# Batch 0 of a fused attention and two-layer feed-forward kernel: VectorE in a written-out order, maxima one tile ahead

## Chip, cores and metric

One core of one Trainium2 chip runs the whole program. The metric is the device time of one execution in microseconds (us); lower is better. Before the change three runs gave 1151.52, 1152.64 and 1152.75 us, a median of 1152.64 us.

## What is computed

Attention with 4 batches, 8 heads, 576 rows and head size 64, in float32, with a threshold on the scores; then two feed-forward layers over the 2304 tokens. Cut to what matters:

```python
scores = (1/8) * q @ k.T                     # 4 x 8 x 576 x 576
m = max(scores, axis=-1)
scores = where(scores >= m - tau, scores, -1e9)
attn = exp(scores - m);  attn /= sum(attn) + 1e-9
x = attn @ v                                 # reshaped to 2304 x 512
g = x @ w_gate;  x = (g * sigmoid(g) * (x @ w_val)) @ w_out      # 512 -> 1536 -> 512
h = max(x @ w_in, 0);  out = (h * h) @ w_out2                    # 512 -> 2048 -> 512
```

## The kernel before, in words

The attention is cut into 144 tiles of 128 query rows by 576 key columns. A pair of heads has 9 tiles and a batch has 4 pairs, so tiles 0 to 35 are batch 0. The main loop (L845 to L895) makes one iteration i for each tile; each tile passes through a chain that spreads over several iterations:

- QK (L599): TensorE makes the scores into one of two PSUM buffers s0 and s1 (L603), four matmuls of 288 columns, eight for the mixed tile of a pair. QK(i+1) is issued in iteration i.
- RED (L621): VectorE takes the row maximum less tau, the threshold (tensor_scalar with an accumulator, seen as TENSOR_SCALAR_CACHE_REDUCE and DVE_READ_ACCUMULATOR, L623).
- CUT (L628): ScalarE applies the threshold (Prelu, L631) from PSUM into the single buffer z. After it the score buffer is free for QK of the tile two further on.
- EXP (L635): ScalarE takes the exponential into one of three buffers e and sums the row (L639).
- RCP (L642): VectorE takes the reciprocal of the sum (L644). NORM (L646): GpSimd multiplies e by it (L649).
- TR (L661): TensorE transposes the five 128-column blocks of e into two PSUM banks (L669). From tile 20 on all tiles use the same two banks.
- PH (L683): the two banks are copied out, in batch 0 one half by VectorE (L55) and one by ScalarE (L53). In batches 1 to 3 ScalarE copies both (L689) and VectorE takes the rest of a two-part split (PL, L701, L61).
- AV (L715): TensorE multiplies by v; in batch 0 five float32 matmuls (L725), later ten (L728), in four of nine iterations.

In iteration i, RED, CUT and EXP are those of tile i, RCP and NORM of tile i-1, TR of tile i-2, PH of tile i-3.

Two other jobs run beside the attention. `pair_steps` (L538) prepares the next pair of heads: loads and moves on the queue of SyncE (SP), two splits on ScalarE, VectorE (L565) and GpSimd. And the class `Loader` (L104) brings in the first five blocks of first-layer weights, 30 pieces of 256 columns: they lie in memory as 64-bit words and are turned into two float32 parts. A piece is a DMA on SP's queue (L128), one absolute value on ScalarE (L137), four steps on VectorE (L139, L141, L145, L147: a tensor_scalar each for the first two, a scalar_tensor_tensor for the others, 256 columns each, all in SBUF), a copy on ScalarE (L53) and a subtraction on GpSimd (L61). `loader.start()` begins a piece, from iteration 8 on in every second iteration and from 36 on in each; at most three are under way, in three buffers. `loader.tick(engine)` (L153) issues the next step of the oldest piece that waits for that engine; a change of engine within a piece needs a new iteration. The loop has four ticks for VectorE in an iteration, two for ScalarE, one for GpSimd.

When batch 0 is done, the first layer's matmuls for its rows are woven into the loop as "fill" (L788): per half batch five units of 24 matmuls (L226), each of which needs four of the 30 pieces, and then an output stage (L271), which needs the last ten pieces.

The program is written in an order, but a scheduler sorts it: each instruction has a priority by its place in the program, `tc.high_priority(offset=n)` (L842) shifts it by n instructions (the tables `early0` for iterations below 36 and `early` above, L1605 and L1612), and an engine that is free in the scheduler's own model gets the ready instruction with the best priority, be it from a later iteration. On the chip each engine then runs its instructions in that order. `tc.issue_after(x)` adds an edge: what is issued inside it comes after x on x's engine.

The parts of the loop that the change touches, as they stand before (arguments cut):

```python
    for i in range(NTILE + lag + 1):
        t = i - lag - 1
...
        at_(loader.tick, "D", name="LD")
        if i < NTILE:
            at_(RED, i); at_(CUT, i)
        if 0 <= t < NTILE:
            at_(PH, t); at_(NEG, t)
        if i < NTILE:
            at_(EXP, i)
        at_(loader.tick, "D", name="LD")
...
        if 0 <= i - 1 < NTILE:
            at_(RCP, i - 1); at_(NORM, i - 1)
        at_(loader.tick, "D", name="LD")
        at_(QK, i + 1); work(i); at_(TR, i - lag)
```

Of the kernel before, what the change touches and what calls it, by code (L numbers as in the profile page):

```python
# [20 lines left out]
B, H, S, D = 4, 8, 576, 64  # L21
# [46 lines left out]
def attention_moe(tc, qkv, qk0, tau, w1, w2, out, cfg):  # L68
    nc = tc.nc
# [103 lines left out]
    loader = Loader()  # L173
# [242 lines left out]
    for i in range(2):  # L416
        t = [ptp.tile([P, P], F32R, name=f"qt{i}{j}", tag=f"qt{i}{j}") for j in range(2)]
# [120 lines left out]
    def pair_steps(p):  # L538

        raw = load_pair(p)  # L540
        land = rawp.tile([P, 2, S], F32R, name=f"land{p}", tag="land")
        q, k = raw[:, 0:S], raw[:, S : 2 * S]
        qh, kh = land[:, 0], land[:, 1]

        def move(h):
            hd = head(h)
            rows = slice(hd["odd"] * D, (hd["odd"] + 1) * D)
            for dst, parts_ in (
                (hd["qs"], (qh, q.bitcast(F32R))),
                (hd["kh"], (kh, kh)),  # L550
                (hd["kl"], (k.bitcast(F32R), k.bitcast(F32R))),
            ):
                for j, src in enumerate(parts_):
                    nc.sync.dma_start(dst[j * D : (j + 1) * D, :].bitcast(F32), src[rows, :].bitcast(F32))
            tail(hd)

        yield None
        if cfg["qs"] == "A":
            nc.scalar.activation(qh, q, AF.Copy, scale=qscale)
        else:  # L560
            nc.gpsimd.tensor_scalar(qh, q, scalar1=qscale, scalar2=1.0, op0=ALU.mult, op1=ALU.mult)
        yield None
        ops.copy(cfg["kh"], kh, k)
        yield None
        nc.vector.scalar_tensor_tensor(  # L565
            q.bitcast(F32R), q, qscale, qh.bitcast(F32), op0=ALU.mult, op1=ALU.subtract
        )
        yield None
        ops.sub(cfg["kl"], k[:, :HS].bitcast(F32R), k[:, :HS], kh[:, :HS].bitcast(F32))
        yield None  # L570
        ops.sub(cfg["kl"], k[:, HS:].bitcast(F32R), k[:, HS:], kh[:, HS:].bitcast(F32))
        move(2 * p)
        yield None
        values(heads[2 * p], 2 * p, raw)
        yield "next"
        move(2 * p + 1)
        yield None
        values(heads[2 * p + 1], 2 * p + 1, raw)
        yield None
# [16 lines left out]
    NTILE = len(tiles)  # L596
    st = [dict() for _ in range(NTILE + 8)]
# [211 lines left out]
    def work(i):  # L809

        fstate["credit"] += cfg["rate"]
        if avq:
            at_(AV, avq.pop(0))
            if fstate["credit"] < cfg["extra"]:
                return
        if fstate["credit"] > 0:
            y = at_(fill_group)
            if y is None:
                fstate["credit"] = 0
            else:  # L820
                fstate["credit"] -= y
# [12 lines left out]
    def at_(f, *args, name=None):  # L834
        if name in ("LD", "LA") and 8 <= fstate["i"] < 16:

            with tc.issue_after(st[1]["red" if name == "LD" else "exp"]):
                return f(*args)
        off = cfg["early0" if fstate["i"] < 9 * NPAIR else "early"].get(name or f.__name__, 0)
        if not off:  # L840
            return f(*args)
        with tc.high_priority(offset=off):  # L842
            return f(*args)

    for i in range(NTILE + lag + 1):  # L845
        mp1.age += 1
        fstate["i"] = i
        t = i - lag - 1
        if i == cfg["three"] + lag:
            mp1.banks = deque(bank[2:])  # L850
        if i >= cfg["ldat"] and (i % cfg["lev"] == 0 or i >= 9 * NPAIR):
            at_(loader.start, name="LS")
        at_(loader.tick, "D", name="LD")
        if i < NTILE:
            at_(RED, i)
            at_(CUT, i)
        if 0 <= t < NTILE:
            at_(PH, t)
            at_(NEG, t)
        if i < NTILE:  # L860
            at_(EXP, i)
        at_(loader.tick, "D", name="LD")
        at_(loader.tick, "A", name="LA")
        at_(mp1.flush, "D", name="FD")
        if 0 <= t < NTILE:
            at_(PL, t)
            if tiles[t][2] in PARTS:
                avq.append(t)
        if 0 <= i - 1 < NTILE:
            at_(RCP, i - 1)  # L870
            at_(NORM, i - 1)
        at_(loader.tick, "D", name="LD")
        at_(mp1.flush, "A", name="FA")
        if i + 1 < NTILE:
            at_(QK, i + 1)
        work(i)
        if 0 <= i - lag < NTILE:
            at_(TR, i - lag)
        at_(mp1.flush, "P", name="FP")
        at_(loader.tick, "P", name="LP")  # L880
        at_(loader.tick, "A", name="LA")
        if i < NTILE:
            b, p, k = tiles[i]
            ha = b * H + 2 * p
            pr = i // 9
            if pr == 0:
                for _ in range((0, 1, 2)[k] if k < 3 else 0):
                    next(first)()
            elif k < 2:
                at_(next, steps, name="PS")  # L890
            if pr + 1 < B * NPAIR and k >= 2:
                if k == 2:
                    steps = pair_steps(pr + 1)
                at_(next, steps, name="PS")
        at_(loader.tick, "D", name="LD")  # L895
    while avq or not fstate["end"]:
        mp1.age += 1
        mp1.flush()
# [10 lines left out]
    f = 0  # L909
# [638 lines left out]
def pack(inputs):  # L1548
# [15 lines left out]
    def cols(w, nf):  # L1564
# [48 lines left out]
        "TR": 8, "LD": -21, "FD": 4, "NEG": -4, "FA": -19, "PL": -12, "PS": -25, "PH": 6, "LS": 64, "RCP": -8,  # L1613
        "FP": -40, "NORM": -25, "LP": -100,
    },
    "rate": 2600,
    "extra": 4000,
    "wl2": "D",
# [6 lines left out]
def program(arrays):  # L1625
    import concourse.bacc as bacc

    nc = bacc.Bacc("TRN2", target_bir_lowering=False, num_devices=1, dynamic_dma_scratch_size=512)
    args = [nc.dram_tensor(n, a.shape, mybir.dt.from_np(a.dtype), kind="ExternalInput").ap() for n, a in arrays]
    out = nc.dram_tensor("out_0_dram", (NT, DM), F32, kind="ExternalOutput").ap()  # L1630
    with tile.TileContext(nc) as tc:
        attention_moe(tc, *args, out, CFG)
    return nc
# [9 lines left out]
```

## Time and profile before

| | us |
|---|---|
| median of three runs | 1152.64 |
| the profiled execution | 1153.14 |
| its span, first to last instruction | 1151.3 |
| PE (TensorE matmul) busy in the span | 1115.7 (97%) |
| DVE (VectorE) busy | 874.8 (76%) |
| ACT (ScalarE) busy | 689.2 (60%) |
| POOL (GpSimd) busy | 242.8 (21%) |
| tile 9's maximum starts | 28.39 |
| tile 38's maximum starts | 109.55 |

The profile is one execution, recorded by the hardware; times count from its first instruction. An instruction of an engine can start a little before the one ahead of it ends, so durations add up to slightly more than the time they take. PE's busy time is modelled at its ends and is not PE at its peak. The granted clock of TensorE was 0.997 of full speed over the span. A busy engine is not always the bound: what matters is which engine the others wait for in that stretch.

### The profile page before, as it was taken

To read this page: it belongs to the slowest core of one execution; us is meant where nothing else is said; L and a number is where in the kernel's file an instruction comes from. 1 tells how busy PE (TensorE), PEld (TensorE's weight loads), DVE (VectorE), ACT (ScalarE), POOL (GpSimd) and SP (SyncE) were. 2 spreads that over 40 slices of the span, in tenths; PEclk is the share of its full clock that TensorE was granted. 3 is DMA by queue.
4 is the path that set the end of the run, shared out by engine and by line. 5 is a ranking of instruction groups with operands and counts; after the bars stand their busy time and mean duration, and the time that the engine had idled before them with its cause. 6 is when DMAs were issued, how large, how long until landed. Compare 5 with 4: busy or idle time off the path is not lost.

```text
span 1151.3 us, 19654 instructions
## 1 busy us (share of the span) xinstructions
PE 1115.7 (97%) x6572; PEld 1011.6 (88%) x6572; DVE 874.8 (76%) x2143; ACT 689.2 (60%) x1626; POOL 242.8 (21%) x363
## 2 busy tenths in 40 slices
PE   7888999999999999999999999989999999999998
PEld 5766989999999999998888888889898998899997
DVE  7999997877877773889986888668648767866554
ACT  7988988988888883554443444235546555543221
POOL 5565664555455531000000000000000000000000
PEclk9999999999999999999999999989999999999999
DMA  6666433443333400332220234246364445444542
GB/s 195 193 178 166 128 99 95 100 120 95 95 95 95 105 22 1 101 93 82 83 74 1 73 131 161 91 143 244 137 210 174 174 157 177 153 155 138 187 171 80
DMA packets 55827, 143.15 MB, mean 124 GB/s; under 512 B 7600, under 2 KB 8880, under 8 KB 55728
## 3 DMA queue, kind: packets, MB, share of 16 engines
q1 hardware_dynamic: 55584, 141.92, 39.8%
q8 instruction: 52, 0.85, 0.3%
q14 instruction: 47, 0.39, 0.1%
q10 hardware_dynamic: 144, 0.00, 0.0%
HBM read 93.06 MB, written 22.28 MB: 100 GB/s over the span
## 4 chain that ended last, share of the span: by engine, by line
PE 76%; DVE 12%; ACT 5%; DMA 2%; issue 2%; POOL 0%; POOLq 0%; DVEq 0%; ACTq 0%; SPq 0%
PE mm L226 17%; PE mm L1453 17%; PE mm L1400 13%; PE mm L271 8%; PE bank L226 6%; PE bank L669 4%; PE s L613 4%; PE bank L271 4%; PE bank L728 4%; DVE st__101 L623 2%; DMA wr<-in_w_dram 1%; ACT z L631 1%; DVE pt L61 1%; ACT e L639 1%; DVE xs_m L61 1%
## 5 line engine op out<-in xcount | busy, mean ns | idle before, releaser
L669 PE MATMUL bank<-ident,e 128*128 128x128 f32 x720 | 165.4, 275 | 10.2 <-DVE x L55 3.8
L649 POOL TENSOR_SCALAR e<-e,r 128x576 f32<-128x576 f32 x144 | 113.4, 787 | 148.1 <-DVE r L644 104.6
L61 DVE TENSOR_TENSOR pt<-bank,pt 128x384 fp32r<-128x384 f32 x216 | 100.3, 486 | 51.1 <-ACT pt L689 49.9
L226 PE MATMUL mm<-xs,wa 128*128 128x512 f32 (+2 forms) x672 | 125.7, 347 | 0.5 <-ACT x L53 0.5
L226 PEld LDWEIGHTS mm<-xs,wa 128*128 128x128 f32 x672 | 109.5, 188 | 15.7 <-ACT x L53 0.7
L631 ACT ACTIVATE z<-s,thr 128x576 f32<-128x576 f32 x144 | 106.8, 742 | 26.5 <-DVE st__101 L623 18.5
L623 DVE TENSOR_SCALAR_CACHE_REDUCE st__101<-s,tau_c 128x576 bf16<-128x576 f32 x144 | 116.6, 810 | 5.2 <-PE s L613 4.2
L669 PEld LDWEIGHTS bank<-ident,e 128*128 128x128 f32 x720 | 96.4, 141 | 21.7 <-DVE x L55 5.9
L226 PE MATMUL bank<-xs_m,wa 128*128 128x288 f32 x576 | 109.7, 327 | 3.7 <-DVE xF L740 1.8
L689 ACT ACTIVATE pt<-bank 128x384 fp32r<-128x384 f32 x216 | 88.7, 436 | 21.5 <-PE bank L669 20.2
L639 ACT ACTIVATE e<-z 128x577 f32<-128x577 f32 x144 | 99.6, 692 | 1.5 <-POOL e L649 0.4
L226 PEld LDWEIGHTS bank<-xs_m,wa 128*128 128x128 f32 x576 | 89.0, 189 | 7.1 <-DVE xs_m L61 2.7
L728 PE MATMUL bank<-pt,vs 128*128 128x256 f32 (+1 forms) x480 | 92.1, 323 | 2.1 <-ACT pt L689 1.4
L613 PE MATMUL s<-kh,qs 128*128 128x288 f32 x256 | 78.1, 319 | 7.4 <-ACT nident L413 5.9
L728 PEld LDWEIGHTS bank<-pt,vs 128*128 128x128 f32 x480 | 73.9, 190 | 3.8 <-ACT pt L689 2.1
L1470 DVE TENSOR_TENSOR xF<-xF,mm 128x512 f32<-128x512 f32 x54 | 37.0, 686 | 50.9 <-PE mm L1453 50.9
L226 PE MATMUL mm<-xs,wb 128*128 128x512 f32 (+1 forms) x360 | 74.9, 368 | 0.0
L613 PE MATMUL s<-kl,qs 128*128 128x288 f32 x256 | 73.7, 301 | 0.0
L226 PEld LDWEIGHTS mm<-xs,wb 128*128 128x128 f32 x360 | 62.9, 188 | 11.3
L53 ACT ACTIVATE wb<-wf 128x256 fp32r<-128x256 f32 x82 | 34.0, 414 | 64.5 <-DVE wf L1057 38.4
L1054 ACT ACTIVATE wf<-wr 128x256 f32<-128x256 f32 x64 | 27.6, 433 | 68.6 <-DMA wr<-in_w_dram 51.0
L1453 PE MATMUL mm<-wb,wx 128*128 128x512 f32 x270 | 67.1, 389 | 0.0
(156 smaller groups left out, 2603.0 us busy)
## 6 DMA issues: line engine op xcount, KB each, us to landing
wr<-in_w_dram SPq DMA_DIRECT2D x106, 256.0 KB, 2.9
raw<-in_qkv_dram SPq DMA_DIRECT2D x15, 896.0 KB, 4.7
kh<-land SPq DMA_DIRECT2D x60, 144.0 KB, 2.6
kl<-raw SPq DMA_DIRECT2D x60, 144.0 KB, 2.8
xF<-in_w_dram SPq DMA_DIRECT2D x30, 256.0 KB, 2.9
right<-kept1T SPq DMA_DIRECT2D x8, 768.0 KB, 5.3
right<-kept0T SPq DMA_DIRECT2D x7, 768.0 KB, 5.3
right<-kept SPq DMA_DIRECT2D x6, 768.0 KB, 5.1
```

The costliest lines, as they stand in the source:

```text
L61: e.tensor_tensor(out, a, b, op=ALU.subtract)
L226: mm(pt[:, :n], w[:, a, col + c * P : col + (c + 1) * P], xs[:, b, c, :], start=(i == 0), stop=(i == len(TERMS) - 1),)
L271: mm(pt[:, :n], w[:, a, 2 * DM + m * P : 2 * DM + (m + 1) * P], u[:, b, :], start=(k == 0), stop=(k == last),)
L613: mm(sp[:, cols], l, r[:, cols], start=(n_ == 0), stop=(n_ == len(pairs) - 1),)
L623: red = nc.vector.tensor_scalar(st_, st[t]["s"][:, :S], scalar1=tau_c, scalar2=None, op0=ALU.subtract, op1=ALU.max, accum_out=th)
L631: nc.scalar.activation(z[:, :S], st[t]["s"][:, :S], AF.Prelu, bias=st[t]["thr"], scale=-1.0, alpha=1 / SLOPE)
L639: ex = nc.scalar.activation(e, st[t]["z"], AF.Exp, scale=-SLOPE, accum_out=sum_)
L649: nc.gpsimd.tensor_scalar(e, e, scalar1=r, scalar2=1.0, op0=ALU.mult, op1=ALU.mult)
L669: mm(dst[:, j], e[:, c0 : c0 + P], ident, is_transpose=True, start=(j == 0), stop=(j == len(cols) - 1),)
L728: mm(o[:, :n], hd["vs"][:, SLOT[k % 5], :], pt[:, k, lo : lo + n], start=(k == 0), stop=(k == 9))
L1400: mm(bank[:, :BK], w[:, a, c * P : (c + 1) * P], t[:, b, c, :], start=(n == 0 and x in ("11", "12", "S1")), stop=(n == 5), skip_group_chec ...
L1453: mm(pt, u[:, b, s * P : (s + 1) * P], w[a], start=(half == 0 and j == 0 and i == 0), stop=(half == 1 and j == 1 and i == 2),)
```

## The change

In iterations 9 to 37 VectorE's attention and loader steps are chained by edges into one order: the reciprocal of tile i-1, the copy of tile i-3, the maximum of tile i+1, and two loader steps. NORM comes right behind the reciprocal. The other two loader ticks are left out in these iterations. The maximum moves from iteration i to iteration i-1, and for it QK of tile i+2 is issued at the end of iteration i, where QK of tile i+1 was issued in its middle. (Tiles 0 to 35 are not split in PH, so NEG issues nothing for them.)

```diff
+    order = {"after": None}
+    def inorder(f, *args, name=None):
+        if order["after"] is None:
+            at_(f, *args, name=name)
+        else:
+            with tc.issue_after(order["after"]):
+                at_(f, *args, name=name)
+        traced = nc.cur_bb.bb.instructions
+        engine = st[0]["red"].engine
+        order["after"] = next(x for x in reversed(traced) if x.engine == engine)
...
-        at_(loader.tick, "D", name="LD")
-        if i < NTILE:
-            at_(RED, i)
+        fixed = cfg["fixed"][0] <= i < cfg["fixed"][1]
+        if fixed:
+            inorder(RCP, i - 1)
+            at_(NORM, i - 1)
+            if i == cfg["fixed"][0]:
+                inorder(RED, i)
             at_(CUT, i)
-        if 0 <= t < NTILE:
-            at_(PH, t)
-            at_(NEG, t)
-        if i < NTILE:
+            inorder(PH, t)
+            inorder(RED, i + 1)
             at_(EXP, i)
-        at_(loader.tick, "D", name="LD")
+            for _ in range(2):
+                inorder(loader.tick, "D", name="LD")
+        else:
...
-        if 0 <= i - 1 < NTILE:
+        if 0 <= i - 1 < NTILE and not fixed:
             at_(RCP, i - 1)
             at_(NORM, i - 1)
-        at_(loader.tick, "D", name="LD")
+        if not fixed:
+            at_(loader.tick, "D", name="LD")
         at_(mp1.flush, "A", name="FA")
-        if i + 1 < NTILE:
+        if i + 1 < NTILE and not fixed and i != cfg["fixed"][1]:
             at_(QK, i + 1)
         work(i)
...
-        at_(loader.tick, "D", name="LD")
+        if cfg["fixed"][0] <= i + 1 <= cfg["fixed"][1]:
+            at_(QK, i + 2)
+        if not fixed:
+            at_(loader.tick, "D", name="LD")
...
+    "fixed": (9, 38),
```

The branch behind `else:` holds the old order, with RED left out in iteration 38, whose maximum iteration 37 has made.

## Rows read from the trace of the kernel before

**Rows 1.** The page's 40 slices of the span: busy tenths of two engines.
```profile
PE   7888999999999999999999999989999999999998
DVE  7999997877877773889986888668648767866554
```

**Rows 2.** Stretches of the first 190 us; the first line names the columns.
```profile
core 0: us, PE busy (x) PEld busy (x) DVE busy (x) ACT busy (x) POOL busy (x), PEclk, DMA share, GB/s
...
28.40:109.55 81.15, 69.69 (x399) 55.87 (x400) 76.37 (x199) 72.68 (x180) 48.15 (x67) 1.00 0.67 185
109.55:138.00 28.45, 27.75 (x204) 26.65 (x204) 27.11 (x76) 26.59 (x67) 17.55 (x26) 1.00 0.49 132
138.00:166.60 28.60, 25.54 (x184) 23.52 (x184) 28.14 (x71) 22.34 (x57) 18.95 (x27) 1.00 0.44 114
166.60:190.00 23.40, 22.98 (x179) 22.47 (x177) 16.28 (x44) 20.26 (x52) 10.83 (x16) 1.00 0.27 58
```

**Rows 3.** VectorE in order of time: start, duration; tile 9 to tile 38.
```profile
27.52 0.95 DVE L147 SCALAR_TENSOR_TENSOR xF<-xF 128x256 int32<-128x256 int32 x1
28.39 0.81 DVE L623 TENSOR_SCALAR_CACHE_REDUCE st__101<-s,tau_c 128x576 bf16<-128x576 f32 x1
...
64.00 0.79 DVE L623 TENSOR_SCALAR_CACHE_REDUCE st__101<-s,tau_c 128x576 bf16<-128x576 f32 x1
...
65.06 0.80 DVE L623 TENSOR_SCALAR_CACHE_REDUCE st__101<-s,tau_c 128x576 bf16<-128x576 f32 x1
...
68.69 0.81 DVE L623 TENSOR_SCALAR_CACHE_REDUCE st__101<-s,tau_c 128x576 bf16<-128x576 f32 x1
...
109.55 0.81 DVE L623 TENSOR_SCALAR_CACHE_REDUCE st__101<-s,tau_c 128x576 bf16<-128x576 f32 x1
```

**Rows 4.** ScalarE by line, 28.4 to 109.5: busy, mean ns | idle before.
```profile
L631 ACT ACTIVATE z<-s,thr 128x576 f32<-128x576 f32 x29 | 21.5, 741 | 5.4 <-DVE st__101 L623 2.8 <-DVE r L644 2.4
L137 ACT ACTIVATE xF<-xF 128x256 f32<-128x256 f32 x12 | 5.3, 441 | 0.0
L53 ACT ACTIVATE wa<-xF 128x256 fp32r<-128x256 f32 x11 | 4.5, 414 | 1.2 <-DVE xF L147 1.2
```

**Rows 5.** The loader's VectorE steps L139, L141, L145, L147 before and behind tile 38.
```profile
0.00:109.55 109.55, 9.37 (x22) 1.00 0.67 188
109.55:166.60 57.05, 3.16 (x8) 1.00 0.47 123
...
0.00:109.55 109.55, 10.70 (x22) 1.00 0.67 188
109.55:166.60 57.05, 4.18 (x8) 1.00 0.47 123
...
0.00:109.55 109.55, 14.62 (x22) 1.00 0.67 188
109.55:166.60 57.05, 6.21 (x9) 1.00 0.47 123
...
0.00:109.55 109.55, 9.83 (x21) 1.00 0.67 188
109.55:166.60 57.05, 3.88 (x9) 1.00 0.47 123
```

**Rows 6.** Loader steps alone, then one beside GpSimd's NORM, in order of time.
```profile
61.31 0.28 DVE L141 TENSOR_SCALAR wf<-wf 128x256 int32<-128x256 int32 x1
...
62.20 0.41 DVE L145 SCALAR_TENSOR_TENSOR wf<-xF,wf 128x256 int32<-128x256 int32 x1
...
67.63 0.87 POOL L649 TENSOR_SCALAR e<-e,r 128x576 f32<-128x576 f32 x1
...
67.91 0.86 DVE L145 SCALAR_TENSOR_TENSOR xF<-xF 128x256 int32<-128x256 int32 x1
```

**Rows 7.** TensorE's first fill matmul, the loader's last step, the first output matmul.
```profile
113.57 0.69 PE L226 MATMUL bank<-xs_m,wa 128*128 128x288 f32 x4
...
166.11 0.41 DVE L147 SCALAR_TENSOR_TENSOR xF<-xF 128x256 int32<-128x256 int32 x1
...
166.85 0.82 PE L271 MATMUL bank<-m_u,wa 128*128 128x288 f32 x5
```

**Rows 8.** SP's queue at the loader's DMAs: waits, ns min/median/max.
```profile
L128 SPq EVENT_SEMAPHORE  x24: 17/88/5037, 19.1 to 139.6; - x24
```

More of the change, by code (lines that the diff above doesn't have):

```diff
@@ L852, in attention_moe @@
             at_(loader.start, name="LS")
-        at_(loader.tick, "D", name="LD")
-        if i < NTILE:
-            at_(RED, i)
+        fixed = cfg["fixed"][0] <= i < cfg["fixed"][1]
[4 more added lines that the diff above has]
+                inorder(RED, i)
             at_(CUT, i)
-        if 0 <= t < NTILE:
-            at_(PH, t)
-            at_(NEG, t)
-        if i < NTILE:
+            inorder(PH, t)
+            inorder(RED, i + 1)
             at_(EXP, i)
-        at_(loader.tick, "D", name="LD")
+            for _ in range(2):
+                inorder(loader.tick, "D", name="LD")
+        else:
+            at_(loader.tick, "D", name="LD")
+            if i < NTILE:
+                if i != cfg["fixed"][1]:
+                    at_(RED, i)
+                at_(CUT, i)
+            if 0 <= t < NTILE:
+                at_(PH, t)
+                at_(NEG, t)
+            if i < NTILE:
+                at_(EXP, i)
+            at_(loader.tick, "D", name="LD")
         at_(loader.tick, "A", name="LA")
@@ L868, in attention_moe @@
                 avq.append(t)
-        if 0 <= i - 1 < NTILE:
+        if 0 <= i - 1 < NTILE and not fixed:
             at_(RCP, i - 1)
             at_(NORM, i - 1)
-        at_(loader.tick, "D", name="LD")
+        if not fixed:
+            at_(loader.tick, "D", name="LD")
         at_(mp1.flush, "A", name="FA")
-        if i + 1 < NTILE:
+        if i + 1 < NTILE and not fixed and i != cfg["fixed"][1]:
             at_(QK, i + 1)
@@ L894, in attention_moe @@
                 at_(next, steps, name="PS")
-        at_(loader.tick, "D", name="LD")
+        if cfg["fixed"][0] <= i + 1 <= cfg["fixed"][1]:
+            at_(QK, i + 2)
+        if not fixed:
+            at_(loader.tick, "D", name="LD")
     while avq or not fstate["end"]:
```

## The prediction, made before the changed kernel was run

> **What bounds the kernel now.** I read the page's 40 slices first, for the places where TensorE is not full. They are the first ten slices or so: PE stands at 7 and 8 tenths in the first four, while DVE stands at 9 in most of them, and behind the attention PE stays at 9 [rows 1]. So the kernel is bound by TensorE except early on, and time is won there alone: a microsecond less of PE's idle time early is a microsecond less at the end, as long as PE finds its work later as before.
>
> Next the stretches [rows 2]. Between the maxima of tile 9 and tile 38, the stretch that the change rewrites, 81.15 us pass for 29 tiles. PE is busy for 69.69 us of them and idle for 11.5; VectorE for 76.37, ScalarE for 72.68. Behind it the picture turns. From 109.55 to 138 PE is busy for 27.75 of 28.45 us, VectorE for 27.11. From 138 to 166.6 VectorE is busy for 28.14 of 28.60 us, PE for 25.54. Only after that does VectorE fall to 16.28 of 23.40.
>
> Then VectorE in order of time [rows 3]. The maxima come in pairs, at 64.00 and 65.06, and the next at 68.69: two tiles, then over three microseconds of other VectorE work. ScalarE, which needs the maximum for CUT, sits idle for 5.4 us in the stretch before its 29 CUTs [rows 4].
>
> What fills VectorE between the pairs is mostly the loader. Up to tile 38 its four lines have 22, 22, 22 and 21 instructions, 87 steps; behind it, to 166.6, 34 at most, one of which starts ahead of the border and is counted twice, so 33 [rows 5]. 87 + 33 = 120, the 30 pieces. The scheduler has run the loader ahead: by the program's own order 14 pieces (56 steps) are due in iterations up to 37, and it has done 87.
>
> **The change, part by part.** The sum is made against the profiled execution, 1153.14 us with a span of 1151.3; the median of three runs lies 0.5 lower. About 0.2%, 2.3 us, is what a measurement of this kernel can tell from no change.
>
> *Loader steps in a fixed order.* No step of the chained iterations can run ahead any more, and an iteration has two. Piece k starts in iteration 8 + 2(k-1), takes its absolute value two iterations on, and its four steps in the next two pairs, 12 + 2(k-1) and the one after. Thirteen pieces fit until iteration 37: 52 steps where 87 ran, 35 fewer. ScalarE loses six of the nineteen pieces it converts in the stretch, at 0.44 + 0.41 us [rows 4]: 5.1 us.
>
> *What that gives.* In the stretch VectorE has 76.37 us of work, less 22 of its 74 steps (76.37 - 22 x 0.52 = 65); ScalarE 72.68 - 5.1 = 67.6; PE its unchanged 69.69. PE is now the longest, so the stretch can't be shorter than that, and the gain at most 11.5 us. Some idle time stays: PE was idle for 1.8% of the stretch 166.6 to 190, where nobody else is full, and for 10.7% of 138 to 166.6 [rows 2]; with these ends the stretch takes 71.0 or 78.0 us. I take 6%, 74.1, nearer the middle because ScalarE at 67.6 is almost as long: 7 us gained, with ends 3 and 10. Ahead of tile 9's maximum stands a loader step from 27.52 to 28.39 that moves behind it [rows 3]: another 0.9. Together **8 us, between 3 and 11**.
>
> *What has to be paid back.* The 35 steps are not gone. The output stage of the fill needs all 30 pieces, and it starts at 166.85, right behind the loader's last step at 166.11 [rows 7]; the first fill matmul needs only four and starts at 113.57, so it is not delayed. Behind tile 38 the loader now has 68 steps in place of 33, on an engine that is 95% and 98% busy there. The price of a step: alone 0.28 or 0.41 us [rows 6], with overlapping ends about 0.27 on average; in that stretch 17.4 us for 34, 0.52 [rows 5]. I take 0.40, between them, since PE waits can open room: 14 us, between 9.5 and 18.2. Off that go VectorE's own idle 1.8 us there (57.05 - 27.11 - 28.14) and a share of the 7.1 us idle from 166.6 to 190 [rows 2], say 3, if the last pieces slip past 166.6: **9 us paid back, between 0.6 and 16.4**.
>
> *The maximum a tile ahead.* It takes away at most ScalarE's 5.4 us of waits [rows 4]; since PE sets the stretch, this is inside the 8 us, not beside it. In its place VectorE now stands at the reciprocal until EXP of the tile before has ended, and the copy of tile i-3, the next maximum and two loader steps queue behind it. VectorE has 65 us of work in some 74, so 9 us of such waiting fit; beyond that TensorE's transposes, which wait for the copies, would be late next.
>
> *QK an iteration sooner.* It is still free only once CUT has read the buffer, and on PE the order stays QK(i+2), work, TR: it stood in the middle of iteration i+1 ahead of that work and now stands at the end of iteration i. Nothing, either way; the score buffer covers it, and without that cover the maximum of the next tile would be late by one QK.
>
> *The queues.* No DMA is added. On SP's queue a loader DMA that waits for its buffer holds up the moves for the next pair behind it; 24 of the 30 have a wait, 0.088 us in the middle and 5.04 at most [rows 8]. Pieces an iteration slower can lengthen such waits; the moves are due an iteration or more later, so I count 0, with a loss of up to 5 in the range. On POOL, NORM comes right behind the reciprocal, ahead of the loader's subtraction as before: 0.
>
> *Collisions.* The same loader step takes 0.41 us alone and 0.86 beside a NORM [rows 6]. In the new order NORM falls beside the copy and the maximum. That cheapens steps inside the chained stretch, where by the sum VectorE is no longer the longest: 0 there. The Trainium skill ("SBUF — State Buffer", Who interferes with whom) has VectorE and GpSimd share a port pair as an exclusive lock, the later one waiting until the first has ended; the two durations agree. By it the 35 steps that move behind tile 38, where GpSimd is not ordered and is busy for 36.5 of 57 us, cost the upper price and the sum would be 5 us worse.
>
> The sum: 1153.1 - 8 + 9 = 1154.1, and 0.5 lower for the median: **1153.6 us**, no difference that can be measured.
>
> **The rivals.**
>
> *Faster: the debt sinks into slack.* From 109.55 to 138 PE is 97.5% busy, so VectorE's time there may not be what the end waits for; attention tiles, which need no weights, could run ahead on PE while the loader catches up, and the last pieces fall into the free 7.1 us. Then 2 us are paid back: 1152.6 - 8 + 2 = **1146.6**. For it: PE's fullness there, and that four pieces are enough to begin. Against it: VectorE is 95% and 98% busy, and the attention's own VectorE work comes first in that queue too.
>
> *Slower: the debt is dearer than the gain.* It is one mechanism, in the stretch 109.55 to 166.6: VectorE is the bound there and each of the 35 moved steps costs its full 0.52 us. 18.2 - 4.8 = 13.4 are paid for a gain of 5 to 6, PE keeping more of its idle time: about +8, **1160**. It decides from a price of (8 + 4.8) / 35 = 0.37 us a step. For it: 98% from 138 on, and the output stage starting right behind the loader. Against it: the first half of that stretch belongs to PE. The Trainium skill ("Perfetto Trace Analysis", Optimization Strategy) says that regimes with different busiest engines may gain by being interleaved; this change pulls loader work out of the one and stacks it in the other, and by that rule this rival comes true. No run here shows it yet.
>
> *The order was about the same already.* Then neither gain nor debt appears, and the time stands at 1152.6. The 87 steps against 52 speak against it; the time would be as in my forecast.
>
> **How the numbers follow.** Gain and debt nearly cancel in my sum, with errors of some 4 us in each: no change (with the last rival) 0.36, faster 0.35, slower 0.29. The likeliest case's own range is 1150.3 to 1154.9. The ends of the bounds are 1152.6 - 11 + 0.6 = 1142 and 1152.6 - 3 + 16.4 = 1166; they need all terms at one end. The range 1145.5 to 1160.5 holds the faster case with a 7 us gain and the slower one with 8, and leaves out about 2 in 10.
>
> **What would show it.** Tile 38's maximum should start at 99 to 104 us instead of 109.55, single maxima some 2.55 us apart instead of pairs, 52 loader steps ahead of it, no idle time of ScalarE for the maximum. Behind it 68 loader steps, VectorE full until the last, the output stage starting at 165 to 170. PE's idle time in the chained stretch should fall to about 4 to 5 us and rise by as much behind. I am wrong if tile 38 doesn't come earlier (the chain blocks VectorE), or if the output stage starts before 160 (the debt was hidden), or after 172 (it was dearer).

## The result and the profile after

The changed kernel is **slower**: a median of 1160.85 us against 1152.08, a ratio of 1.0084 with an interval of 1.0055 to 1.0113 (it is formed from all the runs; the quotient of the two medians is 1.0076). Run once more on another occasion it took 1163.83 against 1152.84, ratio 1.0098 (1.0079 to 1.0117). The forecast was no difference, with a range up to 1160.5.

The profiled execution after took 1166.21 us, with a span of 1164.4. It lies above the median: against the profiled execution before it loses 13.1 us, where the medians differ by 8.8, and a part of what its stretches show is TensorE's clock (last section). The page's 40 slices, as in [rows 1]:

```profile
PE   7988879999999999999999999999999999999998
DVE  5888997877778784789986978778647767866554
```

A slice is 29 us. The second has risen from 8 to 9, the fifth and sixth, 116 to 175 us, have fallen from 9 to 8 and 7: time was won early and lost right behind. To measure both, the stretches are cut where the kernel's own work cuts them: from tile 9's maximum to tile 38's, and from there to the start of the fill's output stage. In the kernel before these are 28.39 to 109.55, as in [rows 2], and 109.55 to 166.85. First that second stretch before, columns as in [rows 2]:

```profile
109.55:166.85 57.30, 53.55 (x388) 50.42 (x388) 55.50 (x146) 49.18 (x124) 36.59 (x53) 1.00 0.47 123
```

The profile after:

```profile
26.80:104.34 77.54, 68.99 (x395) 55.38 (x394) 62.86 (x175) 68.02 (x163) 40.63 (x58) 0.99 0.60 162
104.34:175.10 70.76, 59.90 (x392) 53.12 (x391) 68.78 (x174) 56.82 (x143) 44.76 (x62) 0.97 0.48 142
```

and the profile of the second occasion:

```profile
26.90:103.00 76.10, 69.00 (x399) 55.46 (x398) 62.59 (x175) 67.93 (x163) 40.54 (x58) 1.00 0.61 165
103.00:174.50 71.50, 60.55 (x388) 54.68 (x387) 69.02 (x176) 56.86 (x143) 45.35 (x62) 0.93 0.49 141
```

This is nearly the whole result. In the first stretch VectorE's busy time fell from 76.37 us to 62.86, by 13.5, and the stretch became shorter by only 3.6 (5.1 on the second occasion). In the second, VectorE has 68.78 us where it had 55.50, 13.3 more, and the stretch became longer by 13.5, from 57.3 to 70.8: VectorE is busy for 97% of it, before and after. Work was taken from an engine where it held the stretch only in part and given to it where it is nearly full. Of the 13.5 us, TensorE's idle time makes up 7.1 and its busy time 6.4. The output stage starts at 175.07 instead of 166.85:

```profile
112.03 0.56 PE L226 MATMUL bank<-xs_m,wa 128*128 128x288 f32 x3
...
177.71 0.41 DVE L147 SCALAR_TENSOR_TENSOR xF<-xF 128x256 int32<-128x256 int32 x1
...
175.07 0.56 PE L271 MATMUL bank<-m_u,wa 128*128 128x288 f32 x3
```

These are the lines of [rows 7]: the fill still begins early, 1.5 us ahead of before, but its output stage comes 8.2 us later. From there to the end 989.3 us pass, before 984.4; on the second occasion 987.1.

VectorE's maxima, as in [rows 3], mostly stand alone now: tiles 9 and 10 and tiles 11 and 12 are still 1.2 to 1.3 us apart, and from tile 13 on no two are closer than 1.8 us.

```profile
26.80 0.82 DVE L623 TENSOR_SCALAR_CACHE_REDUCE st__101<-s,tau_c 128x576 bf16<-128x576 f32 x1
...
44.08 0.81 DVE L623 TENSOR_SCALAR_CACHE_REDUCE st__101<-s,tau_c 128x576 bf16<-128x576 f32 x1
...
46.01 0.81 DVE L623 TENSOR_SCALAR_CACHE_REDUCE st__101<-s,tau_c 128x576 bf16<-128x576 f32 x1
...
48.73 0.82 DVE L623 TENSOR_SCALAR_CACHE_REDUCE st__101<-s,tau_c 128x576 bf16<-128x576 f32 x1 [0.36 <-PE s L613]
...
104.34 0.80 DVE L623 TENSOR_SCALAR_CACHE_REDUCE st__101<-s,tau_c 128x576 bf16<-128x576 f32 x1
```

ScalarE's wait for the maximum ahead of CUT, 2.8 us in [rows 4], is 1.2 us in three places:

```profile
L631 ACT ACTIVATE z<-s,thr x29: 725/737/755, 27.7 to 103.0; 128x576 f32<-128x576 f32 x29
...
  DVE st__101 L623: 1.2, 3
```

The loader's four lines, in the order of [rows 5], ahead of tile 38 and behind it:

```profile
26.80:104.30 77.50, 7.57 (x14) 0.99 0.60 162
104.30:178.50 74.20, 8.13 (x16) 0.97 0.46 136
...
26.80:104.30 77.50, 5.50 (x14) 0.99 0.60 162
104.30:178.50 74.20, 7.38 (x16) 0.97 0.46 136
...
26.80:104.30 77.50, 6.08 (x13) 0.99 0.60 162
104.30:178.50 74.20, 10.91 (x17) 0.97 0.46 136
...
26.80:104.30 77.50, 6.25 (x12) 0.99 0.60 162
104.30:178.50 74.20, 9.27 (x18) 0.97 0.46 136
```

14 + 14 + 13 + 12 = 53 steps ahead of tile 38, where 87 were; 67 behind, where 33 were. Behind tile 38 the 67 steps take 35.7 us, where the 33 took 17.4 [rows 5]: 18.3 us for the 34 that changed sides, 0.54 us each. Five of the 67 stand behind the start of the output stage, so the second stretch has 29 more. VectorE's busy time there rose by 13.3 us, 0.46 for each of the 29, less than 0.54 because overlapping ends count only once in it.

Last, who waits in the second stretch. TensorE's waits for VectorE sum up to 2.6 us there in the kernel before and to 7.9 after. The main ones before (us in total, times, longest):

```profile
PE bank L226 <- DVE xF L740: 1.0, 1, 1.0
...
PE bank L669 <- DVE pt L61: 0.7, 2, 0.5
...
PE bank L226 <- DVE xs_m L61: 0.3, 1, 0.3
```

and after, with one that is put down to ScalarE:

```profile
PE bank L226 <- DVE xs_m L61: 2.3, 3, 1.3
PE bank L226 <- DVE xF L740: 2.1, 2, 1.1
PE bank L669 <- DVE pt L61: 2.0, 2, 1.4
...
PE bank L728 <- ACT xF L137: 1.5, 1, 1.5
...
PE bank L728 <- DVE xF L740: 1.3, 1, 1.3
```

No wait of TensorE in this list is for a weight. It waits for VectorE's other work, the fill's inputs (xs_m), the sums of the attention's output (L740) and the split copies (pt), which have the loader's steps between them. The two waits of 1.31 and 0.58 us just ahead of the output stage show it:

```profile
164.25 0.88 DVE L147 SCALAR_TENSOR_TENSOR xF<-xF 128x256 int32<-128x256 int32 x1
...
165.06 0.88 DVE L139 TENSOR_SCALAR xF<-xF 128x256 f32<-128x256 f32 x1
...
165.85 0.70 DVE L61 TENSOR_TENSOR xs_m<-xF,xs_m 128x288 fp32r<-128x288 f32 x1
...
166.48 0.96 DVE L141 TENSOR_SCALAR xF<-xF 128x256 int32<-128x256 int32 x1
...
166.61 0.67 PE L226 MATMUL bank<-xs_m,wa 128*128 128x288 f32 x3 [1.31 <-DVE xs_m L61]
...
167.36 0.44 DVE L61 TENSOR_TENSOR xs_m<-xF,xs_m 128x288 fp32r<-128x288 f32 x1
...
167.85 0.53 PE L226 MATMUL bank<-xs_m,wa 128*128 128x288 f32 x2 [0.58 <-DVE xs_m L61]
```

Three loader steps of 0.88 to 0.96 us stand ahead of and between the xs_m that TensorE waits for. The wait of 1.5 us put down to L137 comes by another way: ScalarE stood for 1.36 us at the copy of a weight piece, until VectorE had done its last step at 132.29, and the attention's copy (pt) stood behind it on ScalarE. So the late steps also reach TensorE through ScalarE's order. PE's idle time in this stretch rose from 3.8 to 10.9 us, and in the first it fell from 11.5 to 8.6.

### The profile page after: what moved, and what is told of

Its sections match the earlier page's. It is cut to its first block, busy times and chain, and to the rows that moved or that the text cites. A ratio compares the mean times of both kernels' runs of the same rounds, so it can differ in the third digit from the quotient of the medians.

```text
span 1164.4 us, 19635 instructions
## 1 busy us (share of the span) xinstructions
PE 1123.2 (96%) x6572; PEld 1014.6 (87%) x6572; DVE 870.6 (75%) x2143; ACT 692.3 (59%) x1626; POOL 242.0 (21%) x363
## 4 chain that ended last, share of the span: by engine, by line
PE 78%; DVE 9%; ACT 5%; DMA 2%; issue 2%; POOLq 0%; POOL 0%; ACTq 0%; DVEq 0%; SPq 0%
PE mm L226 17%; PE mm L1484 16%; PE mm L1431 13%; PE mm L271 9%; PE bank L226 6%; PE s L613 4%; PE bank L669 4%; PE bank L271 4%; PE bank L728 4%; DVE st__101 L623 1%; PE bank L725 1%; ACT z L631 1%; DMA wr<-in_w_dram 1%; DVE pt L61 1%; DMA xF<-in_w_dram 1%
## 5 line engine op out<-in xcount | busy, mean ns | idle before, releaser
L669 PE MATMUL bank<-ident,e 128*128 128x128 f32 x720 | 162.8, 276 | 8.0 <-ACT x L53 3.3
L623 DVE TENSOR_SCALAR_CACHE_REDUCE st__101<-s,tau_c 128x576 bf16<-128x576 f32 x144 | 116.7, 811 | 12.3 <-PE s L613 11.7
L226 PEld LDWEIGHTS mm<-xs,wa 128*128 128x128 f32 x672 | 109.5, 188 | 15.7 <-ACT x L53 0.7
L639 ACT ACTIVATE e<-z 128x577 f32<-128x577 f32 x144 | 99.5, 691 | 3.0 <-POOL e L649 0.4
L1085 ACT ACTIVATE wf<-wr 128x256 f32<-128x256 f32 x64 | 27.6, 433 | 71.5 <-DMA wr<-in_w_dram 53.7
```

What stands on the lines that cost most here:

```text
L226: mm(pt[:, :n], w[:, a, col + c * P : col + (c + 1) * P], xs[:, b, c, :], start=(i == 0), stop=(i == len(TERMS) - 1),)
L623: red = nc.vector.tensor_scalar(st_, st[t]["s"][:, :S], scalar1=tau_c, scalar2=None, op0=ALU.subtract, op1=ALU.max, accum_out=th)
L639: ex = nc.scalar.activation(e, st[t]["z"], AF.Exp, scale=-SLOPE, accum_out=sum_)
L669: mm(dst[:, j], e[:, c0 : c0 + P], ident, is_transpose=True, start=(j == 0), stop=(j == len(cols) - 1),)
```

## The experiments

Theory: the debt. The chain keeps the loader from running ahead, 34 steps land on a full VectorE behind tile 38, and they are the loss. Main rival: the chain itself, a VectorE that stands at a reciprocal or a copy with everything behind it. Further rivals: the earlier scores, and the order without the edges. Each kernel was timed against the kernel before on the same chip.

**The loader out of the chain** (the rest of the order kept):

```diff
             for _ in range(2):
-                inorder(loader.tick, "D", name="LD")
+                at_(loader.tick, "D", name="LD")
```

> The change, with the two loader steps of an iteration taken out of the chain: they may run ahead or behind again, the rest of the order stays. Debt theory (35 loader steps moved behind tile 38 cost the 9 us): over 70 loader steps ahead of tile 38, output stage before 168 us, time 1147 to 1154. Chain theory (the written order itself stalls VectorE): 1158 to 1163 as with the change.

Measured 1151.04 us, ratio 0.9983 (0.9974 to 0.9993). 94 loader steps ahead of tile 38, output stage at 166.1. The two stretches:

```profile
28.87:108.12 79.25, 68.91 (x400) 55.77 (x400) 73.15 (x204) 72.97 (x184) 49.01 (x67) 1.00 0.68 192
108.12:166.13 58.01, 53.90 (x387) 50.28 (x387) 54.38 (x139) 49.07 (x123) 37.47 (x54) 1.00 0.45 118
```

VectorE is back at 73 and 54 us, near the 76 and 56 of the kernel before, and the loss is gone. The order of maximum, copy and reciprocal can stay chained without it.

**The kernel before, with its loader held back:**

```diff
+        held = 9 <= i < 38
...
+        if held:
+            with tc.issue_after(st[i]["red"]):
+                for _ in range(2):
+                    at_(loader.tick, "D", name="LD")
```

(the four old ticks are issued only where `held` is false)

> The kernel before, with its own order, but in iterations 9 to 37 the loader has two VectorE ticks and each comes behind that iteration's maximum. Debt theory: 50 to 60 loader steps ahead of tile 38, output stage behind 172 us, time 1157 to 1163. Chain theory: nothing of the attention's order has changed, so 1151 to 1154.

Measured 1161.45, ratio 1.0077 (1.0062 to 1.0092), with 61 steps ahead of tile 38 and the output stage at 171.6:

```profile
27.00:108.31 81.31, 71.95 (x409) 58.19 (x408) 68.64 (x186) 70.97 (x172) 44.36 (x62) 0.98 0.58 159
108.31:171.60 63.29, 55.51 (x373) 50.19 (x374) 61.94 (x161) 52.44 (x133) 41.19 (x57) 0.97 0.51 148
```

No edge touches the attention here and its program text is the old one, and the loss is about that of the whole change. With the run before it this shows that holding the loader back is what costs. The amounts differ: VectorE lost 7.7 us of work in the first stretch and nothing was gained there, while the second grew by 6.0 us and what stands behind it by 2.7. TensorE's lower clock cost some 1.6 and 1.9 us in the two stretches (estimates from the means of 0.98 and 0.97). The output stage was expected behind 172 and came 0.4 us ahead of that; the steps, expected at 50 to 60, came to 61.

**Both kernels without the loader's VectorE steps**, so that the order stands alone:

```diff
-            yield "D"
-            nc.vector.tensor_scalar(fl, fl, scalar1=F64_MIN, scalar2=None, op0=ALU.max)
+            if self.phase:
+                yield "D"
+                nc.vector.tensor_scalar(fl, fl, scalar1=F64_MIN, scalar2=None, op0=ALU.max)
```

(and so for the other three steps)

> The kernel before without the loader's four VectorE steps for the first 30 pieces (those weights are left unconverted). Both theories: VectorE loses some 60 us of work up to 166 us and PE's idle time there falls: 1132 to 1146.

> The changed kernel without the loader's four VectorE steps for the first 30 pieces (those weights are left unconverted). Debt theory: without a debt the written order shows its gain alone, 2 to 6 us below the same cut of the kernel before. Chain theory: 4 us or more above it.

Measured 1140.43 for the kernel before (ratio 0.9895, 0.9877 to 0.9912) and 1142.29 for the changed one (0.9916, 0.9894 to 0.9938). The expectation of a gain failed, and the intervals overlap: no gain of the written order shows. The stretch from tile 9 to 38, before and then changed:

```profile
26.81:101.78 74.97, 69.77 (x410) 57.01 (x409) 43.99 (x124) 72.78 (x190) 47.74 (x69) 1.00 0.75 207
```

```profile
26.90:103.12 76.22, 69.20 (x408) 56.65 (x406) 43.00 (x125) 73.16 (x191) 48.02 (x71) 1.00 0.75 210
```

With VectorE busy for 44 us the stretch still takes 75 to 76, so here it is ScalarE (73) and PE (70) that keep it from being shorter. The changed kernel, at 76.1 to 77.5, stood near that; whether the same floor holds for it, with 68 us of ScalarE and not 73, was not tried.

**The chain with more loader steps.** Four a round, and a piece begun in every iteration:

```diff
-        if i >= cfg["ldat"] and (i % cfg["lev"] == 0 or i >= 9 * NPAIR):
+        if i >= cfg["ldat"]:
...
-            for _ in range(2):
+            for _ in range(4):
                 inorder(loader.tick, "D", name="LD")
```

> The changed kernel with the chain kept, but a piece begun in every iteration and four loader steps chained in each, so that the loader keeps step though it can't run ahead. Debt theory: 75 to 100 loader steps ahead of tile 38, its start back at 107 to 112 us, output stage before 169, time 1150 to 1155. Chain theory: as the change, 1158 or more.

Measured 1167.57, ratio 1.0130 (1.0115 to 1.0145): a miss by more than 12 us.

```profile
26.89:126.39 99.50, 80.24 (x401) 60.70 (x400) 90.90 (x231) 79.33 (x193) 49.79 (x72) 0.91 0.59 165
126.39:181.91 55.52, 54.04 (x397) 51.40 (x395) 48.05 (x128) 47.34 (x118) 34.63 (x51) 1.00 0.43 111
```

108 steps ahead of tile 38, more than the 87 of the kernel before, and now the first stretch has become long. In the second PE is 97% busy and VectorE 87%: what was taken off VectorE there is worth little. For this run alone the rival holds: 116 steps without the chain (next) cost 0.5%, 108 with it 1.3%. With four steps the chain does cost something of its own, only part of it TensorE's clock, 0.91 in the first stretch (below): at whole-run clocks of 0.989 and 0.992 the kernel without the chain took 1160.3 and 1160.0 us, this one at 0.991 from 1167.3 to 1169.8. With the change's two steps the two runs above show no such cost.

**More steps without the chain**, in the written order and in the kernel before: the same two edits, with `at_` for `inorder`; and the first of the two alone.

> The written order with the loader out of the chain, a piece begun in every iteration and four ticks. If running ahead is worth the 0.4 us a step that the debt costs, more than 94 steps stand ahead of tile 38 and the time is 1146 to 1151; if VectorE is already full up to tile 38, steps only change places and it is 1150 to 1153.

> The kernel before with a piece begun in every iteration from 8 on. Zero-sum reading (VectorE is the bound from tile 9 to the loader's end, so it doesn't matter when its steps run): more steps ahead of tile 38, tile 38 later, 1150 to 1154.

Measured 1158.85 (ratio 1.0047, 1.0029 to 1.0066) with 116 steps ahead of tile 38, and 1157.66 (1.0036, 1.0022 to 1.0050) with 114. Both expectations failed. The stretches of the second, whose clock was full:

```profile
28.54:115.61 87.07, 69.45 (x400) 56.10 (x400) 84.47 (x224) 76.68 (x191) 53.33 (x71) 1.00 0.65 183
115.61:169.39 53.78, 52.52 (x388) 50.32 (x388) 46.04 (x121) 46.67 (x114) 33.07 (x49) 1.00 0.44 112
```

Here it is the other way round. VectorE is busy for 97% of the first stretch, which grows by 5.9 us; the second shrinks by 3.5 and stops at PE's 52.5. Zero-sum was the wrong reading: work can be pushed too far forward as well as too far back. The size is small, though. This profile, the kernel's fastest execution (1153.87), has 2.4 us more in the two stretches together and 1.9 less behind them; the other four, at whole-run clocks of 0.994 to 0.997, took 1155.9 to 1158.1. The kernel before took 1151.6 to 1151.8 at full clock on that chip, so some 2 us of the loss stay at full clock, and the rest of the median's 4.5 goes with the clock.

**Three chained steps, pieces begun in two of three iterations:**

```diff
-        if i >= cfg["ldat"] and (i % cfg["lev"] == 0 or i >= 9 * NPAIR):
+        if i >= cfg["ldat"] and (i % 3 or i >= 9 * NPAIR):
...
-            for _ in range(2):
+            for _ in range(3):
```

> The chain with three loader steps an iteration, and pieces begun in two of three iterations. Balance reading: 70 to 85 steps ahead of tile 38 as in the kernel before, and 1152 to 1156 if the number of steps alone decides; over 1158 if the chained order leaves PE idle whatever the number, as it did with four.

Measured 1160.14, ratio 1.0073 (1.0057 to 1.0088), but with 58 steps ahead of tile 38, not 70 to 85; perhaps because the loader has three pieces under way at most and chained steps keep them long, which was not followed. So it does not separate the two readings. It is one more point at a low number of steps, and the one least disturbed by the clock:

```profile
27.72:105.39 77.67, 71.37 (x410) 56.86 (x408) 65.10 (x183) 69.82 (x170) 43.09 (x60) 1.00 0.63 173
105.39:174.41 69.02, 56.71 (x375) 50.62 (x376) 67.82 (x171) 53.83 (x136) 42.06 (x59) 0.98 0.47 133
```

The first stretch is 3.5 us shorter than in the kernel before, the second 11.7 longer, with VectorE busy for 98% of it; TensorE's waits for VectorE there sum up to 10.3 us.

**No edges at all**, the reordered text alone (`at_` for every `inorder`):

> The change without any edge: the reordered program text (reciprocal and NORM first, maximum of tile i+1, two loader ticks, scores an iteration sooner), but the scheduler may run the loader ahead. Debt theory: VectorE's idle time from tile 9 to the output stage 6 to 11 us, time 1149 to 1153. If the edges only fix what the order alone does, 1157 or more.

Measured 1150.95, ratio 0.9985 (0.9974 to 0.9996), 87 steps ahead of tile 38, VectorE idle for 9.6 us from tile 9 to the output stage. The reordering costs nothing; the edges do.

**The scores an iteration sooner, alone**, in batch 0 and then in all batches:

```diff
-        if i + 1 < NTILE:
+        if i + 1 < NTILE and not 9 <= i <= 38:
             at_(QK, i + 1)
...
+        if 9 <= i + 1 <= 38:
+            at_(QK, i + 2)
```

> The kernel before with one part of the change alone: in iterations 8 to 37 the scores of tile i+2 are issued at the end of iteration i. Debt theory: PE's order stays, 1151 to 1154. Rival, the earlier scores cost: 1156 or more.

> The kernel before with the scores issued an iteration sooner in all iterations from 8 on, not in batch 0 alone. If the 2 us that this part gave in batch 0 come from scores that are ready sooner, 1147 to 1151; if they were a chance of the schedule, 1150 to 1156.

Measured 1150.81, ratio 0.9980 (0.9970 to 0.9989), and 1150.05, ratio 0.9979 (0.9969 to 0.9989). Both beat the kernel before by 0.2% and the changed one by 1%. The first ran a little below its expectation; the second lies in both of its ranges and so does not tell them apart. The first one's stretches:

```profile
28.22:108.14 79.92, 69.62 (x402) 56.35 (x402) 72.11 (x200) 72.44 (x181) 49.11 (x66) 1.00 0.68 186
108.14:164.24 56.10, 52.97 (x384) 50.10 (x385) 53.91 (x145) 48.63 (x124) 36.46 (x52) 1.00 0.48 128
```

88 steps ahead of tile 38, as before, but VectorE needs 126.0 us for the two stretches and not 131.9; a loader step takes 0.47 us on average where it took 0.52. Why the steps collide less in this schedule was not tried. In all batches the part gives no more than in batch 0 alone, and the kernels with the free loader or without edges, which hold this part too, gain no more either. So the one useful part of the change seems to be this one, though that the others add nothing is read from equal medians, not shown.

**The changed kernel again:**

> The changed kernel once more, for a profile with fewer stretches of TensorE's low clock than the first one had. If the pushed-back loader steps are the cause, tile 38 and the output stage stand where the first profile has them, each earlier by 1.7 us for a low stretch of 3.4 us that is missing ahead of it: tile 38 at 102 to 104 us, output stage 171 to 175, time 1158 to 1162.

Measured 1163.83 (above). Tile 38 stands at 103.0 and the output stage at 174.5, as expected; the time is 2 us above its range. This time the low clock fell into the second stretch (0.93).

All kernels, by the loader steps ahead of tile 38:

| steps | kernel | ratio to before |
|---|---|---|
| 53 | changed (two occasions) | 1.0084, 1.0098 |
| 58 | three chained steps | 1.0073 |
| 61 | before, loader held | 1.0077 |
| 87 | before | 1 |
| 87, 88, 88, 94 | no edges; scores sooner (2); loader free | 0.9985, 0.9980, 0.9979, 0.9983 |
| 108 | chained, four steps | 1.0130 |
| 114, 116 | begun each iteration: before; free | 1.0036, 1.0047 |

## Why the prediction was wrong

The forecast was no change, and the rival that came true was "the debt is dearer than the gain", at its own 1160. The prediction had named the sign for it, an output stage behind 172 us; it started at 175.1 and 174.5. Step by step:

- *What bounds the kernel* held in the main: of the 13.1 and 10.3 us that the two profiled executions lose, 8.2 and 7.7 arise ahead of the output stage.
- *Loader steps in a fixed order*: 52 forecast ahead of tile 38, 53 measured; 34 moved, not 35. VectorE's 65 us and ScalarE's 67.6 in the stretch came out as 62.9 and 68.0.
- *What that gives*: 7 us in the stretch from 74.1 us, measured 3.6 and 5.1 from 77.5 and 76.1, inside the ends of 71 to 78. With tile 9's 1.6 and 1.5 us it is 5.2 to 6.5 instead of 8. The step took 6% of the stretch as PE's idle time; measured were 11% and 9%. The kernels without loader steps point to why: even with VectorE half empty, ScalarE's 73 us and PE's 70 took 75.
- *What has to be paid back* is the step that failed: 9 us forecast, while the second stretch grew by 13.5 (14.2 on the second occasion). The term that was too small is the price of a step. 0.40 us was taken, below the 0.52 of the kernel before, "since PE waits can open room". They did not: behind tile 38 the steps cost 0.53 us (35.7 us for 67), and the 34 that moved are 18.3 us and not 14. Even counted by VectorE's busy time, with overlapping ends counted once, it is 0.46. Then 4.8 us were taken off for slack. Of VectorE's own idle 1.8 us nothing came: it is idle for 2.0 us in the longer stretch. Behind the output stage's start 2.1 us came, five steps. And the output stage does not wait for the loader's end, as the step had it: it starts 2.6 us ahead of the last loader step here, and in the run with the free loader 14 us behind it (151.9 and 166.1). What was late was VectorE's other work, with the loader's steps between.
- *The maximum a tile ahead*: its 5.4 us of ScalarE's waits, of which 2.8 were for the maximum, were counted as inside the 8 us. Without the loader's steps no gain of the order shows.
- *QK an iteration sooner*: 0 forecast, a gain of 2.3 us measured alone, right at the bound of what can be told.
- *The queues*: no loss was seen from SP's queue.
- *Collisions*: 0 inside the chained stretch holds, but for another reason. The steps there cost 25.4 us for 53, 0.48 each, so the written order did not take the collisions out. GpSimd's other work, the loader's own subtraction and the next pair's splits, is still there beside them. Behind tile 38 the steps cost the upper price, 0.53, as the prediction had it by the Trainium skill's rule ("SBUF — State Buffer", Who interferes with whom) that VectorE and GpSimd share a port pair as an exclusive lock. The rows from 164 to 168 us above agree with that rule: the three steps take 0.88 to 0.96 us there, with GpSimd busy for 5.4 us of the 6 from 163 to 169. That GpSimd is the cause was not tried. The prediction put this case at 5 us worse than its sum; by its own figures it is 18.2 less 14, so 4.

The rival was given 0.29, with a price of 0.52 a step as its condition. The condition held, and so did its terms: 13.4 us paid for a gain of 5 to 6, measured 13.5 and 14.2 for 5.2 and 6.5. (Its 13.4 is 18.2 less the same 4.8 of slack; in the runs it is 18.3 less overlapping ends and the five steps behind.) The bound was in the text too: it decides from 0.37, and even the 0.40 that was taken lies above that, so the forecast stood on a low price and the slack together. That the rival's +8 also meets the medians (+8.8 and +11.0) is in part luck: no term of it holds the time lost behind the start of the output stage, or the clock. The Trainium skill's advice to interleave regimes with different busiest engines ("Perfetto Trace Analysis", Optimization Strategy) agrees with these runs in both directions, at 53 to 61 steps and at 108 to 116.

Open: the 4.9 and 2.6 us that the changed kernel loses behind the start of the output stage. 1.7 us of it in the first profile is a low-clock stretch. In both, ten more matmuls stand behind that start than in the kernel before (5693 and 5683 in the profiles); at that stretch's mean of 0.17 us they are an estimated 1.7 us. The rest was not followed.

## What to carry to other kernels

Filler work that a scheduler has spread over two stretches can be near a balance already: here 87 to 94 of 120 steps in the first were best, and both fewer and more cost time. Before pinning an order, count where each step of the filler will land, and price it at what such steps take in that very stretch (here 0.53 us, where a step alone takes 0.28 or 0.41); take nothing off for the last per cents of an engine that is 97% busy there. In this kernel the critical chain could be ordered by edges at no cost, as long as the filler was left free.

## What the runs showed of the hardware

TensorE's granted clock fell to its lower level, 1.2 GHz, in stretches that ran at full clock in the kernel before: 0.91 as a mean over 99.5 us in the chain with four steps, 0.93 over 71.5 us in the second look at the change. The same work then keeps PE busy longer: in the first case 401 matmuls took 80.2 us, in the kernel before 399 took 69.7. In the changed kernel's first profile the clock is 0.68, 0.50 and 0.97 in the 2 us stretches from 170 to 176; ahead of it PE had waited for 1.31, 0.58 and 1.06 us, between 165.3 and 169.45. Idle time in a stretch does not settle it: the kernel before with pieces begun in each iteration left PE idle for 17.6 of 87.1 us and kept the full clock in the execution that was profiled, while its other four had 0.994 to 0.997 over the whole run.

So a part of the loss of a kernel that starves TensorE can come from the clock. In the changed kernel's two profiles, at 0.97 and 0.93 in the second stretch, that is some 2 and 5 us of PE's time, and in three chained steps (0.98) only 1.4, with about the same loss; these are estimates, the share of the clock that is missing times the stretch. The changed kernel still took 1159.8 us at a whole-run clock of 0.998, so the loss is not the clock's alone.
